# Idle products in TensorE's pauses at the end of a decode step, and the last K transposes and score maximum in halves

## The chip, the cores and the metric

The kernel runs on one core of a Trainium2 chip. Times are microseconds of device time for one execution of the whole program; lower is better.

## The reference

A decode step of one token for a batch of 4, as a sum of the input, an attention block and a gated MLP, both on the layer-normed input:

```python
def _A_ref(x, k_cache, v_cache, wq, wo):          # x (4,1,640)
    q = (x @ wq).reshape(B, Sq, 32, 128).transpose(0, 2, 1, 3)
    scores = einsum('bhqd,bhkd->bhqk', q, k_cache) * 128 ** -0.5   # caches (4,32,4096,128) bf16
    o = einsum('bhqk,bhkd->bhqd', softmax(scores), v_cache)
    return o.transpose(0, 2, 1, 3).reshape(B, Sq, 32 * 128) @ wo   # wo (4096,640)

def _B_ref(x, w_in, w_sp, b_sp, w_out):           # hidden 864 of 1728
    z = gelu(einsum('bsd,df->bsf', x, w_in))
    g = einsum('ts,bsf->btf', w_sp, layernorm(z[..., 864:])) + b_sp
    return einsum('bsf,fd->bsd', z[..., :864] * g, w_out)

return x + _A_ref(layernorm(x), ...) + _B_ref(layernorm(x), ...)
```

Nearly all data is the K and V caches, each 134 MB, read once.

## The kernel before

The 32 heads are cut into four groups of eight. A unit is one group of one batch element: 8.4 MB of K or of V, held in SBUF as 128 rows of 256 positions. There are 16 K units and 16 V units. All loads of units go through SyncE's queue, one instruction a unit (two for the last K unit of the first group and for the last V unit), in a written order: K of the first four, then V and K in turn, and three V units at the end. SBUF has five half-unit places in the tile `kv`; a table says which two each unit gets, and a load waits until what was there has been read.

A K unit is worked off in eight steps (`emit_K`). Each step transposes 32 by 32 blocks with VectorE (`kT`, line 420), and then TensorE multiplies them with the queries (line 431) into the scores `S`, a PSUM tile of two banks (index `i`), with `w` for the two bf16 halves of a word and `e` for two column groups. After the fourth batch element of a group comes `softmax`: `softmax_max` takes the largest score over both banks (line 438), spreads it over the partitions with a product at line 442 and makes its negative; ScalarE takes the exponential (line 476), VectorE transposes the result (line 482), and `z_fill` lays it out on VectorE, ScalarE and GpSimd as stationary operands. `emit_V` then runs 64 products of 512 columns into a PSUM tile `O` (line 503), four of them side by side on the array, and VectorE reduces them to `R`.

At the end, after the last V unit, `emit_sel` gathers `R` by head with eight products (line 527) into a tile of the pool `misc`, which has two buffers; `emit_oT` scales it and writes `oT` with VectorE (line 536). Then come the products with wo (`o_mul`, line 544): 32 chunks, loaded into the place of the next to last V unit in five pieces that end at chunks 12, 20, 28, 31 and 32. The first 20 chunks go into `proj`, the accumulator that already holds the other summands, 320 columns a product, two column groups side by side. VectorE copies and adds `proj`'s parts (lines 582 and 586) while the last twelve chunks go into a second accumulator, `last`, 160 columns a product, 48 products. One addition (line 596) and two stores end the kernel.

Of the kernel before, what the change touches and what calls it, by code (L numbers as in the profile page):

```python
# [9 lines left out]
ALU = mybir.AluOpType  # L10
AX = mybir.AxisListType
F32 = mybir.dt.float32
# [4 lines left out]
def kernel(  # L17
# [19 lines left out]
    nc = tc.nc  # L37
    P = 128
    B, Sq, D = A_x.shape
    _, H, Sk, Dh = A_k_cache.shape  # L40
# [6 lines left out]
    T = Sk // M  # L47
    C2 = 2
    TC = 32
    KW = Dh // 2  # L50
    assert T == C2 * 4 * TC and M == 16 and KW == 64 and H % HG == 0
    NG = H // HG
    NU = NG * B
# [16 lines left out]
    NH = 2  # L70
    NO2 = NOUT // NH
# [4 lines left out]
    small = ctx.enter_context(tc.tile_pool(name="small", bufs=2))  # L76
# [11 lines left out]
    def misc_ps(shape, dtype):  # L88
        misc_ctr[0] += 1
        return ps_m.tile(shape, dtype, tag="misc", name=f"misc{misc_ctr[0]}")  # L90
# [13 lines left out]
    Zb = [w.bitcast(BF16).rearrange("p (a h c) -> p a h c", h=HG, c=4) for w in w_part[2:4]]  # L104
# [66 lines left out]
    def unit(item, t0, t1):  # L171

        s0, s1 = place[item]
        assert s1 == s0 + 1 or t1 <= T // 2 or t0 >= T // 2
        if t0 >= T // 2:
            return at_slot(s1, (t1 - t0) * Dh, t0 * Dh - SL)
        return at_slot(s0, (t1 - t0) * Dh, t0 * Dh)
# [11 lines left out]
    CW = H * Dh // P  # L189
    RQ = Dh // CW  # L190
    wo_t = at_slot(0, CW * NOUT).rearrange("p (c n) -> p c n", c=CW)
# [8 lines left out]
    ident_bf = const.tile([P, P], BF16)  # L200
# [47 lines left out]
    for q in range(4):  # L248
# [10 lines left out]
    SelX = const.tile([P, RQ, HG * RQ], F32)  # L259
# [3 lines left out]
                          in_=SelH[:, None, :].to_broadcast((P, RQ, HG)))  # L263
# [8 lines left out]
    for q in range(4):  # L272
        nc.gpsimd.tensor_copy(out=SelE[32 * q:32 * q + 32, :, q % 2, :],
                              in_=b8[32 * q:32 * q + 32, 8:8 + HP, None].to_broadcast((32, HP, RQ)))
# [10 lines left out]
                          in_=ident_f[:].rearrange("p (q x c) -> p q x c", q=2, c=C2))  # L285


    proj = ps_j.tile([64, 512], F32)
    RW = NH * B
    for hf in range(NH):  # L290
        nc.tensor.matmul(proj[0:32, 0:NO2], lhsT=ident_bf[:XR, 1 - hf:33 - hf],  # L291
                         rhs=x_bf[:, hf * NO2:(hf + 1) * NO2], start=(hf == 0), stop=False)
# [4 lines left out]
    for hf in range(2):  # L297
        for c in range(DC):
            for j in range(NG):
                n0 = j * HG * Dh + hf * 512  # L300
                nc.tensor.matmul(q4_ps[32 * j:32 * j + 32, hf * 512:hf * 512 + 512], lhsT=xnT[:, c, :],  # L301
                                 rhs=wq[:, c, n0:n0 + 512], start=(c == 0), stop=(c == DC - 1))
# [4 lines left out]
    for a in range(2):  # L307
        op = nc.vector.tensor_copy if a == 0 else nc.scalar.copy
# [14 lines left out]
    for (bk, q), names in z_in.items():  # L323
        col, parts = 0, []
        for t in names:
            p0, p1, st, _, n, k, run = PC[t]
            x0, x1 = max(p0, 32 * q), min(p1, 32 * q + 32)
            m = len(range(x0, x1, st)) * n
            assert col + m <= 256
            src = w_z[:, :, :, f_of[t][0]:f_of[t][1]].rearrange("p d a (r i c) -> p d a r i c", i=k, c=run)  # L330
            dst = zr_ps[bk][32 * q:32 * q + 32, :, col:col + m]
# [11 lines left out]
    for c in range(DC):  # L343
        for parts in z_parts:
            for j, (dst, src) in enumerate(parts):
                nc.tensor.matmul(dst, lhsT=xnT[:, c, :], rhs=src[:, c], start=(c == 0 and j == 0),  # L346
                                 stop=(c == DC - 1 and j == len(parts) - 1))
# [4 lines left out]
    for (bk, q, t), (col, m, n, c0, x0, x1, st) in z_at_col.items():  # L352
        rows = slice(32 * q, 32 * q + 32)
        nc.scalar.activation(out=zT[rows, :, c0:c0 + n, x0:x1:st],  # L354
                             in_=zr_ps[bk][rows, :, col:col + m].rearrange("p a (x c) -> p a c x", c=n),
# [37 lines left out]
    for f0 in range(0, FC, 4):  # L393
        for hf in range(NH):
            for fc in range(f0, min(f0 + 4, FC)):
                nb = 32 if fc == 1 and hf == 0 else RW
                u0, r0 = 32 * fc + 1 - hf, 32 * (fc % 2)
                nc.tensor.matmul(proj[r0:r0 + nb, 0:NO2], lhsT=uT[:, u0:u0 + nb],  # L398
                                 rhs=w_out[:, fc, hf * NO2:(hf + 1) * NO2],
                                 start=(fc == 1 and hf == 0), stop=False)  # L400
# [9 lines left out]
    state = {}  # L410

    def emit_K(u, k):

        g, b = divmod(u, B)
        hh = first.get(u, 0) ^ (k // 4)
        qp, kh = k // 2 % 2, k % 2
        t0 = 2 * TC * (2 * hh + qp)
        kw = unit(("k", u), t0, t0 + 2 * TC).bitcast(F32).rearrange("p (t w) -> p t w", w=KW)[:, :, 32 * kh:32 * kh + 32]
        kT = kT_t[:, k % 2]
        nc.vector.transpose(kT.rearrange("p (t r) -> p t r", r=32), kw)  # L420
        if ("S", g) not in state:
            S_new = ps_s.tile([P, 2, TC, M], F32, tag="S", name="S")
            state[("S", g)] = S_new
        S_ps = state[("S", g)]
        kb = kT.bitcast(BF16).rearrange("p (i t e m w) -> p i t e m w", i=2, e=NE, m=M, w=2)
        w0 = 8 - (b * C2 + hh)
        for w in range(2):
            for i in range(2):
                for e in range(NE):
                    q = 2 * qp + e  # L430
                    nc.tensor.matmul(S_ps[32 * q:32 * q + 32, i], lhsT=QZ[:, b, 2 * kh + w, e, w0:w0 + 32],  # L431
                                     rhs=kb[:, i, :, e, :, w], start=(b == 0 and k < 4 and kh == 0 and w == 0),
                                     stop=(b == B - 1 and k >= 4 and kh == 1 and w == 1))

    def softmax_max(g):
        S_ps = state[("S", g)]
        m1 = small.tile([P, 1], F32, tag="m1")
        nc.vector.tensor_reduce(out=m1[:], in_=S_ps[:].rearrange("p i t m -> p (i t m)"), axis=AX.X, op=ALU.max)  # L438
        dg = ppool.tile([P, P], F32, tag="p", name="dg")
        nc.vector.tensor_scalar(out=dg[:], in0=IdF[:], scalar1=m1[:, 0:1], scalar2=None, op0=ALU.mult)  # L440
        mm = misc_ps([P, P], F32)
        nc.tensor.matmul(mm[:], lhsT=ones_f[:], rhs=dg[:], start=True, stop=True)
        mp = small.tile([P, NE * HP * B], F32, tag="mp")
        nc.vector.tensor_reduce(out=mp[:], in_=mm[:].rearrange("p (x c) -> p x c", c=4), axis=AX.X, op=ALU.max)
        mo = small.tile([P, NE * HP * B], F32, tag="mo")
        nc.vector.tensor_tensor(out=mo[:], in0=mp[:], in1=SelN[:].rearrange("p e x -> p (e x)"), op=ALU.mult)
        negmax = small.tile([P, 1], F32, tag="negmax")
        nc.vector.tensor_reduce(out=negmax[:], in_=mo[:], axis=AX.X, op=ALU.add)  # L448
        return negmax
# [45 lines left out]
    def emit_V(v):  # L495
        g, b = divmod(v, B)
        O_ps = ps_o.tile([P, 4, Dh], F32, tag="O", name="O")
        vv = unit(("v", v), 0, T)

        parts = [(qp, x) for x in range(C2) for qp in range(2)] if v == 0 else [(qp, x) for qp in range(2) for x in range(C2)]  # L500
        for w in [w for qp, x in parts for w in range(32 * x + 16 * qp, 32 * x + 16 * qp + 16)]:
            q = w % 4
            nc.tensor.matmul(O_ps[32 * q:32 * q + 32, :, :], lhsT=Zb[b % 2][:, w].rearrange("p h c -> p (h c)"),  # L503
                             rhs=vv[:, w * 4 * Dh:(w + 1) * 4 * Dh], start=(w < 4), stop=(w >= NW - 4))

        if b == 0:
            R_new = small.tile([P, B, Dh], F32, tag="R", name="R", bufs=1)
            state["R"] = R_new
        R = state["R"][:, b, :]
        if v < NU - 1:  # L510
            om4 = ppool.tile([P, 4, Dh], F32, tag="p", name="om4")
            nc.vector.tensor_tensor(out=om4[:], in0=O_ps[:], in1=Mk4[:, :, None].to_broadcast((P, 4, Dh)), op=ALU.mult)  # L512
            nc.vector.tensor_reduce(out=R, in_=om4[:].rearrange("p c d -> p d c"), axis=AX.X, op=ALU.add)  # L513
        else:
            nc.vector.tensor_scalar(out=R, in0=O_ps[:, 0, :], scalar1=Mk4[:, 0:1], scalar2=None, op0=ALU.mult)  # L515
            for c in range(1, 4):
                nc.vector.scalar_tensor_tensor(out=R, in0=O_ps[:, c, :], scalar=Mk4[:, c:c + 1], in1=R,
                                               op0=ALU.mult, op1=ALU.add)
        if b + 2 < B:
            z_fill(g, b + 2)  # L520

    def emit_sel(g):

        ox = misc_ps([P, B, CW], F32)
        r0 = 32 * g
        for d in range(RQ):
            nc.tensor.matmul(ox[r0:r0 + 32], lhsT=SelX[:, d], rhs=state["R"][:, :, d * CW:(d + 1) * CW],  # L527
                             start=(d == 0), stop=(d == RQ - 1))
        state[("ox", g)] = ox

    oT = const.tile([P, CW * RW + 32], BF16)
# [8 lines left out]
    def o_mul(dst, c, hf, n0, n1, start, stop):  # L540

        nb = 32 if start else RW
        c0 = RW * c + 1 - hf
        nc.tensor.matmul(dst[0:nb, 0:n1 - n0], lhsT=oT[:, c0:c0 + nb], rhs=wo_t[:, c, n0:n1], start=start, stop=stop)  # L544

    fill_qz(0)
    for w in w_part[2:4]:
# [3 lines left out]
    for i, item in enumerate(seq):  # L551
# [6 lines left out]
        g, b = divmod(u, B)  # L558
# [11 lines left out]
                softmax(g)  # L570
        else:
            emit_V(u)
    emit_sel(NG - 1)
    emit_oT(NG - 1)

    CL = 20
    for c in range(0, CL, 2):
        for hf in range(NH):
            for p in range(2):
                o_mul(proj[32 * p:32 * p + 32], c + p, hf, hf * NO2, (hf + 1) * NO2, False, c == CL - 2 and hf == NH - 1)  # L580
    o_1 = ppool.tile([32, NO2], F32, tag="p", name="o_1")
    nc.vector.tensor_copy(out=o_1[:], in_=proj[0:32, 0:NO2])
    NQ = NO2 // 2
# [5 lines left out]
    for c in range(CL, CW):  # L589
        for hf in range(NH):  # L590
            for k in range(2):
                n0 = hf * NO2 + k * NQ
                o_mul(last[32 * k:32 * k + 32], c, hf, n0, n0 + NQ, c == CL and hf == 0, c == CW - 1 and hf == NH - 1)

    o_bf = ppool.tile([64, NQ], BF16, tag="p", name="o_bf")
    nc.vector.tensor_tensor(out=o_bf[:], in0=last[:], in1=o_q[:], op=ALU.add)
# [31 lines left out]
```

## Time and profile before

| | |
|---|---|
| median of 3 runs | 663.94 us (663.32 to 664.98) |
| the profiled execution: own time, span | 664.68 us, 662.8 us |
| busy: PE, DVE, ACT, POOL | 291.6, 371.6, 74.8, 76.4 us |
| data moved, mean rate | 282.60 MB, 426 GB/s |
| mean granted TensorE clock | 0.722 |
| K transposes (L420), 128 of them | 282.6 us, 2274 ns each |
| score products (L431), 1024 | 187.9 us |
| V products (L503), 1024 | 76.3 us |
| largest score (L438), 4 | 4.9 us, 1225 ns each |

The span runs from the first to the last instruction of the program that the profiler recorded; the own time is that of the same execution as the device reports it, and is 1.88 us longer. Busy times say how long an engine worked, not whether anything waited for it. The granted clock is the share of TensorE's clock pulses that were let through.

### The profile page before, as it was taken

How to read it: one execution, taken by the hardware profiler on the slowest of the kernel's cores; microseconds unless marked ns; L12 is line 12 of the kernel's file. 1: busy time of each engine (PE TensorE's matmuls, PEld its weight loads, DVE VectorE, ACT ScalarE, POOL GpSimd, SP SyncE). 2: the span in 40 equal slices, each digit the busy share in tenths (PEclk: the TensorE clock that was granted, in tenths of full speed). 3: DMA queues.
4: the chain of work that ended last, by engine and by line, in shares of the span. 5: the costliest groups of instructions: out<-in, count | busy, mean ns of one | idle time of the engine just before them, and what ended most of it. 6: DMA issues, size and time to landing. Idle time of an engine off the chain costs nothing.

```text
span 662.8 us, 5648 instructions
## 1 busy us (share of the span) xinstructions
PE 291.6 (44%) x2361; PEld 112.0 (17%) x2361; DVE 371.6 (56%) x304; ACT 74.8 (11%) x144; POOL 76.4 (12%) x136
## 2 busy tenths in 40 slices
PE   0436566447063452536344270644426064436254
PEld 0222211112021120112111020211102021112023
DVE  5239999756191744779173461978446191773011
ACT  0310000431000000060200000052200000026100
POOL 7440000031100000030300000022300000004100
PEclk9857879768587685877768586767859577686567
DMA  9999999999999999999999999999999999999996
GB/s 370 443 442 440 410 448 421 435 440 443 424 439 420 435 440 427 432 425 435 436 435 432 435 431 436 427 432 424 436 443 431 432 423 428 443 440 435 410 420 256
DMA packets 6370, 282.60 MB, mean 426 GB/s; under 512 B 1036, under 2 KB 1172, under 8 KB 1304
## 3 DMA queue, kind: packets, MB, share of 16 engines
q1 hardware_dynamic: 5950, 281.60, 98.5%
q0 software_dynamic: 368, 0.65, 0.3%
q8 instruction: 18, 0.29, 0.2%
q14 instruction: 6, 0.05, 0.0%
q10 hardware_dynamic: 28, 0.01, 0.0%
HBM read 282.25 MB, written 0.01 MB: 426 GB/s over the span
## 4 chain that ended last, share of the span: by engine, by line
DMA 69%; DVE 12%; issue 12%; PE 4%; POOL 1%; ACT 1%; SPq 0%; DVEq 0%; POOLq 0%; ACTq 0%
DMA kv<-in_A_k_cache_dram 58%; DVE w_words L420 11%; DMA kv<-in_A_wo_dram 4%; DMA kv<-in_A_v_cache_dram 4%; DMA kv<-in_B_w_in_dram 4%; PE O L503 2%; PE proj L398 1%; PE last L544 1%; POOL kv L382 0%; PE misc L346 0%; ACT kv L354 0%; DVE w_words L482 0%; PE S L431 0%; POOL z_b L384 0%; DVE w_words L464 0%
## 5 line engine op out<-in xcount | busy, mean ns | idle before, releaser
L420 DVE STREAM_TRANSPOSE w_words<-kv 128x2048 f32<-128x2048 f32 x128 | 282.6, 2274 | 132.5 <-DMA kv<-in_A_k_cache_dram 130.3
L431 PE MATMUL S<-w_words,QZ 128*32 128x512 bf16 x1024 | 187.9, 500 | 259.6 <-DVE w_words L420 259.6
L431 PEld LDWEIGHTS <-QZ 128*32 128x32 bf16 x1024 | 59.8, 110 | 384.4 <-issue 338.1
L503 PE MATMUL O<-kv,w_words 128*32 128x512 bf16 x1024 | 76.3, 463 | 44.3 <-DMA kv<-in_A_v_cache_dram 29.1
L468 ACT ACTIVATE w_words<-w_words,MkE 32x128 bf16<-32x128 bf16 x120 | 61.0, 508 | 87.5 <-PE O L503 74.2
L512 DVE TENSOR_TENSOR om<-O,Mk 128x512 f32<-128x512 f32 x15 | 10.4, 692 | 82.7 <-PE O L503 82.6
L466 POOL TENSOR_SCALAR w_words<-w_words,MkE 32x128 bf16<-32x128 bf16 x60 | 42.9, 715 | 109.2 <-PE O L503 104.5
L476 ACT ACTIVATE w_words<-S,negmax 128x1024 bf16<-128x1024 f32 x4 | 4.5, 1113 | 423.8 <-DVE negmax L448 423.8
L503 PEld LDWEIGHTS <-w_words 128*32 128x32 bf16 x1024 | 33.9, 113 | 86.7 <-issue 56.4
L406 POOL COPY QZ<-qT 32x32 bf16<-32x32 bf16 x16 | 5.0, 316 | 286.1 <-PE S L431 285.5
L464 DVE TENSOR_SCALAR w_words<-w_words,MkE 32x128 bf16<-32x128 bf16 x76 | 25.4, 334 | 2.4
L513 DVE TENSOR_REDUCE R<-om 128x128 f32<-128x512 f32 x15 | 15.3, 1020 | 0.5
L487 POOL TENSOR_SCALAR rs<-MkB,rowsum 128x4 f32<-128x4 f32 x4 | 1.2, 297 | 122.2 <-ACT w_words L476 122.2
L482 DVE STREAM_TRANSPOSE w_words<-w_words 128x1024 bf16<-128x1024 bf16 (+1 forms) x8 | 9.6, 1241 | 5.9 <-ACT w_words L476 5.9
L398 PE MATMUL proj<-w_words,z_b 128*8 128x320 bf16 (+1 forms) x52 | 5.7, 398 | 8.8 <-DVE z_b L385 8.8
L438 DVE TENSOR_REDUCE m<-S 128x1 f32<-128x1024 f32 x4 | 4.9, 1225 | 6.2 <-PE S L431 6.2
L527 PE MATMUL misc<-R,SelX 128*32 128x128 f32 x32 | 4.2, 276 | 7.2 <-DVE R L513 5.5
L515 DVE TENSOR_SCALAR R<-O,Mk 128x128 f32<-128x128 f32 x1 | 0.3, 350 | 12.4 <-PE O L503 12.4
L301 PE MATMUL q<-kv,xnT 128*32 128x512 bf16 x40 | 3.9, 567 | 6.3 <-DVE xnT L228 6.3
L544 PEld LDWEIGHTS <-oT 128*8 128x8 bf16 (+1 forms) x88 | 5.0, 109 | 5.5 <-issue 4.2
L490 PE MATMUL misc<-rs,SelE 128*32 128x4 f32 x8 | 1.1, 206 | 10.7 <-POOL rs L487 10.7
L291 PE MATMUL proj<-kv,ident_bf 8*32 8x320 bf16 x2 | 0.7, 442 | 10.6 <-DMA kv<-in_A_x_dram 10.6
(100 smaller groups left out, 87.7 us busy)
## 6 DMA issues: line engine op xcount, KB each, us to landing
kv<-in_A_k_cache_dram SPq DMA_DIRECT2D x2, 4096.0 KB
kv<-in_A_v_cache_dram SPq DMA_DIRECT2D x1, 6144.0 KB
kv<-in_A_wq_dram SPq DMA_DIRECT2D x1, 5120.0 KB, 16.2
kv<-in_A_wo_dram SPq DMA_DIRECT2D x2, 1280.0 KB
kv<-in_B_w_in_dram SPq DMA_DIRECT2D x1, 2160.0 KB, 23.8
kv<-in_A_v_cache_dram SPq DMA_DIRECT2D x1, 2048.0 KB
kv<-in_A_wo_dram SPq DMA_DIRECT2D x1, 1920.0 KB, 22.2
kv<-in_A_wo_dram SPq DMA_DIRECT2D x1, 480.0 KB, 25.5
```

The lines of the kernel that those rows point to most:

```text
L398: nc.tensor.matmul(proj[r0:r0 + nb, 0:NO2], lhsT=uT[:, u0:u0 + nb], rhs=w_out[:, fc, hf * NO2:(hf + 1) * NO2], start=(fc == 1 and hf == 0) ...
L406: nc.gpsimd.tensor_copy(out=QZ[r0:r0 + 32, :, :, :, 8 + 8 * hp], in_=qT[32 * g:32 * g + 32, NE * hp:NE * hp + NE].rearrange("p e a b -> p ...
L420: nc.vector.transpose(kT.rearrange("p (t r) -> p t r", r=32), kw)
L431: nc.tensor.matmul(S_ps[32 * q:32 * q + 32, i], lhsT=QZ[:, b, 2 * kh + w, e, w0:w0 + 32], rhs=kb[:, i, :, e, :, w], start=(b == 0 and k < ...
L464: nc.vector.tensor_scalar(out=dst, in0=src, scalar1=mk, scalar2=None, op0=ALU.mult)
L466: nc.gpsimd.tensor_scalar(out=dst, in0=src, scalar1=mk, scalar2=None, op0=ALU.mult)
L468: nc.scalar.activation(out=dst, in_=src, func=ACT.Copy, scale=mk)
L482: nc.vector.transpose(pT_t[:, j0:j1, :], blocks)
L503: nc.tensor.matmul(O_ps[32 * q:32 * q + 32, :, :], lhsT=Zb[b % 2][:, w].rearrange("p h c -> p (h c)"), rhs=vv[:, w * 4 * Dh:(w + 1) * 4 * ...
L512: nc.vector.tensor_tensor(out=om4[:], in0=O_ps[:], in1=Mk4[:, :, None].to_broadcast((P, 4, Dh)), op=ALU.mult)
L513: nc.vector.tensor_reduce(out=R, in_=om4[:].rearrange("p c d -> p d c"), axis=AX.X, op=ALU.add)
L544: nc.tensor.matmul(dst[0:nb, 0:n1 - n0], lhsT=oT[:, c0:c0 + nb], rhs=wo_t[:, c, n0:n1], start=start, stop=stop)
```

## The change

- `keep_busy` issues products of 512 columns from the identity and the last V unit into a PSUM tile `idle` that nothing reads: four behind the last V product, two behind the selecting products, four behind the chunk before 12 and five behind the chunk before 20. `tc.issue_after` fixes the order on TensorE: each is queued behind the product named, and the following real products behind the last of them.
- For the last step of the last batch element of each group, `emit_K` transposes in two halves, and the products of the first bank are issued between the two.
- `softmax_max` takes the maximum of each bank by itself into `m2` and then the larger of the two.

```diff
@@ emit_K
         kT = kT_t[:, k % 2]
-        nc.vector.transpose(kT.rearrange("p (t r) -> p t r", r=32), kw)
+        kT_v = kT.rearrange("p (i t r) -> p i t r", i=2, r=32)
+        halves = b == B - 1 and k == 7
+        if not halves:
+            nc.vector.transpose(kT.rearrange("p (t r) -> p t r", r=32), kw)
...
-        for w in range(2):
-            for i in range(2):
+        for x in range(2):
+            if halves:
+                nc.vector.transpose(kT_v[:, x], kw[:, TC * x:TC * x + TC])
+            for y in range(2):
+                w, i = (y, x) if halves else (x, y)
                 for e in range(NE):
@@ softmax_max
-        nc.vector.tensor_reduce(out=m1[:], in_=S_ps[:].rearrange("p i t m -> p (i t m)"), axis=AX.X, op=ALU.max)
+        m2 = small.tile([P, 2], F32, tag="m2")
+        for i in range(2):
+            nc.vector.tensor_reduce(out=m2[:, i:i + 1], in_=S_ps[:, i].rearrange("p t m -> p (t m)"), axis=AX.X, op=ALU.max)
+        nc.vector.tensor_tensor(out=m1[:], in0=m2[:, 0:1], in1=m2[:, 1:2], op=ALU.max)
@@ the end (emit_V and emit_sel keep their last product in state["mm"], o_mul returns its product)
-    emit_sel(NG - 1)
+    idle = misc_ps([P, 4 * Dh], F32)
+
+    def keep_busy(n, behind):
+
+        for _ in range(n):
+            with tc.issue_after(behind.ins):
+                behind = nc.tensor.matmul(idle[:], lhsT=ident_bf[:], rhs=unit(("v", NU - 1), 0, T)[:, 0:4 * Dh],
+                                          start=True, stop=True)
+        return behind
+
+    behind = keep_busy(4, state["mm"])
+    with tc.issue_after(behind.ins):
+        emit_sel(NG - 1)
+    behind = keep_busy(2, state["mm"])
     emit_oT(NG - 1)
...
-                o_mul(proj[32 * p:32 * p + 32], c + p, hf, hf * NO2, (hf + 1) * NO2, False, c == CL - 2 and hf == NH - 1)
+                with tc.issue_after(behind.ins):
+                    behind = o_mul(proj[32 * p:32 * p + 32], c + p, hf, hf * NO2, (hf + 1) * NO2, False,
+                                   c == CL - 2 and hf == NH - 1)
+        if c + 2 in (12, CL):
+            behind = keep_busy(4 if c + 2 < CL else 5, behind)
...
-                o_mul(last[32 * k:32 * k + 32], c, hf, n0, n0 + NQ, c == CL and hf == 0, c == CW - 1 and hf == NH - 1)
+                with tc.issue_after(behind.ins):
+                    behind = o_mul(last[32 * k:32 * k + 32], c, hf, n0, n0 + NQ, c == CL and hf == 0,
+                                   c == CW - 1 and hf == NH - 1)
```

More of the change, by code (lines that the diff above doesn't have):

```diff
@@ L502, in emit_V @@
             q = w % 4
-            nc.tensor.matmul(O_ps[32 * q:32 * q + 32, :, :], lhsT=Zb[b % 2][:, w].rearrange("p h c -> p (h c)"),
+            state["mm"] = nc.tensor.matmul(O_ps[32 * q:32 * q + 32, :, :], lhsT=Zb[b % 2][:, w].rearrange("p h c -> p (h c)"),
                              rhs=vv[:, w * 4 * Dh:(w + 1) * 4 * Dh], start=(w < 4), stop=(w >= NW - 4))
@@ L526, in emit_sel @@
         for d in range(RQ):
-            nc.tensor.matmul(ox[r0:r0 + 32], lhsT=SelX[:, d], rhs=state["R"][:, :, d * CW:(d + 1) * CW],
+            state["mm"] = nc.tensor.matmul(ox[r0:r0 + 32], lhsT=SelX[:, d], rhs=state["R"][:, :, d * CW:(d + 1) * CW],
                              start=(d == 0), stop=(d == RQ - 1))
@@ L543, in o_mul @@
         c0 = RW * c + 1 - hf
-        nc.tensor.matmul(dst[0:nb, 0:n1 - n0], lhsT=oT[:, c0:c0 + nb], rhs=wo_t[:, c, n0:n1], start=start, stop=stop)
+        return nc.tensor.matmul(dst[0:nb, 0:n1 - n0], lhsT=oT[:, c0:c0 + nb], rhs=wo_t[:, c, n0:n1], start=start, stop=stop)
     fill_qz(0)
```

## The prediction

> **What bounds the kernel now.** I read the page's slices first, then the chain of waits for the end, then the timeline of TensorE there, and last the windows view cut along the steps of the granted clock. The row of DMA digits:
>
> ```profile
> DMA  9999999999999999999999999999999999999996
> ```
>
> All slices but the last are full: the kernel streams 282.6 MB at 426 GB/s, and what is not behind the last landing is hidden. The chain of waits from 630 us on:
>
> ```profile
> 631.44 0.43 issue
> 631.87 24.71 DMA kv<-in_A_wo_dram
> 656.58 0.04 issue
> 656.62 3.40 PE last L544 x48
> 660.02 0.02 issue
> 660.05 0.32 DVE o_bf L596
> ```
>
> The third piece of wo lands at 656.58; then 48 products (3.40 us), one addition, the store. The fourth and fifth pieces land at 657.77 and 658.16 (the trace's landing events). So after the last byte has landed there are 1.9 us of products still to run. The timeline of TensorE, with the idle time in brackets:
>
> ```profile
> 650.43 1.80 PE L544 MATMUL proj<-kv,oT 128*8 128x320 bf16 x24 [1.07 <-DMA kv<-in_A_wo_dram]
> 653.53 1.26 PE L544 MATMUL proj<-kv,oT 128*8 128x320 bf16 x16 [1.29 <-DMA kv<-in_A_wo_dram]
> 656.62 3.39 PE L544 MATMUL last<-kv,oT 128*32 128x160 bf16 x48 [1.84 <-DMA kv<-in_A_wo_dram]
> ```
>
> The proj products take 320 columns in 75 ns each (1.80/24), the last ones 160 columns in 71 ns each (3.39/48): half the width, the same time. The windows view says why (columns: us, busy time and count of PE, PEld, DVE, ACT, POOL, then granted clock, DMA share, GB/s):
>
> ```profile
> 645.43:648.84 3.41, 1.79 (x29) 1.06 (x22) 1.40 (x4) 0.00 (x0) 0.00 (x0) 1.00 1.02 427
> 648.84:652.25 3.41, 2.32 (x29) 1.48 (x28) 0.31 (x1) 0.00 (x0) 0.00 (x0) 1.00 1.00 419
> 652.25:655.67 3.42, 1.26 (x16) 0.77 (x16) 0.80 (x3) 0.00 (x0) 0.00 (x0) 1.00 0.99 411
> 655.67:659.08 3.41, 2.46 (x38) 2.46 (x39) 0.31 (x1) 0.00 (x0) 0.00 (x0) 0.50 0.27 105
> 659.08:662.49 3.41, 0.93 (x14) 0.59 (x10) 0.32 (x1) 0.00 (x0) 0.00 (x0) 0.50 0.01 2
> ```
>
> The clock steps only on a grid of 3.41 us. It was 1.00 for the proj products and 0.50 for the last 48, and the window before the step had TensorE busy for 1.26 us, 37%. Windows earlier in the trace give the limits:
>
> ```profile
> 502.07:505.48 3.41, 1.60 (x13) 0.43 (x9) 3.41 (x2) 0.00 (x0) 0.00 (x0) 1.00 0.84 365
> 505.48:508.90 3.42, 2.00 (x16) 0.76 (x15) 2.48 (x2) 0.00 (x0) 0.00 (x0) 1.00 1.24 537
> ...
> 543.03:546.44 3.41, 1.54 (x12) 0.43 (x8) 3.41 (x2) 0.00 (x0) 0.00 (x0) 1.00 0.84 365
> 546.44:549.85 3.41, 3.13 (x24) 1.16 (x27) 0.23 (x1) 0.00 (x0) 0.00 (x0) 0.50 1.16 500
> ...
> 594.23:597.64 3.41, 2.04 (x20) 0.89 (x24) 3.09 (x11) 3.26 (x7) 0.00 (x0) 0.50 0.84 365
> 597.64:601.05 3.41, 3.41 (x36) 1.44 (x32) 2.49 (x7) 3.23 (x8) 1.50 (x3) 0.50 1.20 519
> 601.05:604.46 3.41, 0.86 (x16) 0.23 (x8) 1.71 (x2) 3.26 (x7) 3.05 (x5) 1.00 0.80 346
> ```
>
> At full clock a window with 1.60 us busy (47%) keeps it, one with 1.54 (45%) loses it; at half clock 2.04 (60%) does not bring it back, 3.41 does. All windows of the trace fit: full clock is held from about 45% on, and regained from about 82%.
>
> **Part 1, the fifteen idle products.** Each is 512 columns over the whole array. The nearest row is the attention-times-V products (L503), four of which share the array: a group of four starts every 0.216 us at full clock and every 0.427 at half. So a filler costs 0.216 or 0.427. At full clock, in the order of the queue:
> - Four behind the last V product: its issue ends at 646.52, the four run to 647.39. The selecting products wait for VectorE's R until 648.30: hidden, 0.9 us to spare.
> - Two behind the selecting products: 649.17 to 649.6, and the next product waits for wo's first piece, landed at 650.39: hidden.
> - Four behind chunk 11: 652.06 to 652.93, and the second piece lands at 653.49: hidden, 0.5 us to spare.
> - Five behind chunk 19: 654.62 to 655.70, and the third piece lands at 656.58: hidden, 0.9 us to spare. VectorE's copy of proj waits for the real product ahead of them.
>
> With a drain of 0.17 us each, the window 652.25 to 655.67 gets 1.26 + 0.85 + 0.89 = 3.0 us busy, 88% instead of 37%, and the two before it 78% and 81%. So the clock stays at 1.00 at 655.67.
>
> The last 48 then go at full clock. The proj pairs start every 0.135 us for 320 columns, so 160 columns give 0.069 us a pair, 34.6 ns each. Bounds: at best this, at worst the 66.7 ns they take now, should something other than columns pace them; I take 34.6 since the products into misc at L346 were issued at 36 ns each (80 in 2.9 us) even at half clock, each with its own weights. Then 32 products: 656.62 + 1.11 = 657.73; wait for the fourth piece, 657.81; 12 products to 658.22; the fifth piece has landed; 4 products, the last starting at 658.33 and taking 0.23 (0.299 of a proj product less 0.067 for 160 columns): 658.56. Now the last one ends at 660.01. Gain 1.45 us, and it can't pass 1.6, as four products, 0.1 of starts and 0.23 of drain stand behind the landing at 658.16.
>
> A rule of the Trainium skill speaks against this price: "TensorE: Matmul & The Clock Gate", Back-to-back issue gap, gives some 81 ns a product for a stream of weight load and matmul at 128 columns. By it the 48 would take 3.9 us and nothing would be gained; the trace disagrees, with 71 ns now at half clock and 36 ns at L346.
>
> **Part 2, the last K transposes in halves.** One of 2.17 us becomes two of about 1.1, four times in the kernel. Four products for the first half run under the second transpose, and four instead of eight stand behind it: 1.13 us becomes about 0.6. **Part 3, the largest score in halves.** From the rows of 128 elements (0.29) and 1024 (1.23) a reduce of 512 is 0.69; the first runs beside the second four products, then 0.69 and a small op of 0.19 (as L446). Transposes' end to maximum: now 585.62 to 588.05, 2.43 us; then some 0.1 for the second start, 0.04 + 0.69 + 0.03 + 0.69 + 0.03 + 0.19, 1.8 us. Bounds 1 us saved to 0.5 lost, should the halves still wait for each other. On the path: nothing. All it can bring forward is the first V product of the group, which ends at 601.95 and frees the place for a V load; that load is queued behind one that lands at 606.7, a cover of 4.7 us. If that cover were gone, each such us would cost one us, four times. ScalarE, GpSimd and VectorE's later work only start sooner, with no transfer to collide with.
>
> **Sum.** Profiled execution: span 662.8, own time 664.68, so 1.88 lies around it. 664.68 - 1.45 = **663.2**. This execution is 0.74 above the median of 663.94. The grid does not start with the kernel. If I shift it through one period and apply the two limits to the same intervals, the before kernel keeps the full clock at the end in about half of the positions, as an estimate; the runs from 663.32 to 664.98, 1.66 apart, look like both kinds. The change should bring all runs to the kind of the fastest: 0.7 below the median, or 0.1%.
>
> **Rivals.**
> 1. *Something other than columns paces the last 48.* A weight load shows 87 ns at full clock in the proj stage; if two loads in one column group could not overlap, a pair takes 0.087 and the 48 end at 658.9 (gain 1.1); if issue binds at today's 67 ns, the gain is 0. Time 663.6 to 664.7. Against it: L346. 10%.
> 2. *There is no clock to be won*, because only gaps of a whole window cost it, and the step at 655.67 had another cause, or the timed runs mostly hold the clock already. Time 663.9, the median. Against: gaps of 1.07, 1.29 and 1.84 us were followed by 0.50. The same page's section on HAM oscillation asks only for no gap over some 3.4 us; by that rule these gaps cost nothing, which this trace contradicts with its 37% window. 14%.
> 3. *Slower: the fillers run at half clock ahead of the real products.* If the clock falls before chunk 19 ends, five take 2.13 us, from 654.62 to 656.75, and hold back products that were free at 656.62; the four after chunk 11 end 0.24 late too. All 48 are slow as now: 664.68 + 0.15 = 664.8, 0.9 above the median. It decides if the granted clock is 0.50 between 652 and 655.7. To pass 0.3% it would need 2 us, ten times that. 5%.
> 4. *More than 0.3% faster*: under 661.95, which the landing at 658.16 forbids unless the stream itself ends over a us sooner. 6%.
>
> The forecast has the remaining 65%. A measurement of this kernel tells some 0.3%, 2.0 us, from no change; the forecast and the first three rivals all lie inside. So: within 0.3% 0.87, faster 0.09 (rival 4 and the lucky end of the forecast), slower 0.04 (rival 3 with a disturbed stream). The range runs from 0.5 below the forecast, for the spread of the landings, to 664.3, which takes in rival 2 and most of rival 1.
>
> **What would show it.** Right: granted clock 1.00 up to the store; the group of 48 from 3.39 to about 1.9 us, its last products waiting for the landing of wo and not for TensorE; the fillers inside the old idle gaps; span near 661.3; V loads landing as before although the scores' maximum is ready about 0.6 us sooner. Wrong: clock 1.00 with a pair still at 0.13 us (rival 1); clock 0.50 at the last 48 (rivals 2, 3); a start of those 48 after 656.62 by the landing's clock (rival 3); a slice of DMA under 9 in mid-kernel.

## The result, and the profile after

The changed kernel takes 663.33 us (median of 13 runs, 662.26 to 663.66); the kernel before, run beside it, 664.88 (13 runs, 663.32 to 665.95). The ratio is 0.9977, with a 95% interval of 0.9969 to 0.9986: 1.5 us, 0.2%, within the 0.3% of the forecast and on the side it named. The profiled execution has a span of 660.6 and its own time is 662.51.

The chain of waits at the end, as shown for before:

```profile
631.12 24.74 DMA kv<-in_A_wo_dram
655.86 0.04 issue
655.90 1.93 PE last L553 x48
657.83 0.02 issue
657.86 0.32 DVE o_bf L624
```

Two numbers moved: the 48 products take 1.93 us instead of 3.40, and the third piece of wo lands at 655.86 instead of 656.58. The first is the clock. The timeline of TensorE (line 588 is the idle products; one record of the five is missing):

```profile
647.80 1.06 PE L536 MATMUL misc<-R,SelX 128*32 128x128 f32 x8 [0.64 <-DVE R L526]
...
649.73 1.80 PE L553 MATMUL proj<-kv,oT 128*8 128x320 bf16 x24 [0.33 <-DMA kv<-in_A_wo_dram]
651.46 1.04 PE L588 MATMUL misc<-kv,ident_bf 128*128 128x512 bf16 x4
652.82 1.25 PE L553 MATMUL proj<-kv,oT 128*8 128x320 bf16 x16 [0.33 <-DMA kv<-in_A_wo_dram]
654.24 1.03 PE L588 MATMUL misc<-kv,ident_bf 128*128 128x512 bf16 x4 [0.16 <-issue]
655.90 1.92 PE L553 MATMUL last<-kv,oT 128*32 128x160 bf16 x48 [0.64 <-DMA kv<-in_A_wo_dram]
```

Each group of fillers ends before the landing that the next real products wait for: the gaps in brackets before real products still end with DMA or VectorE, never with an idle product. The windows on this execution's grid:

```profile
650.33:653.74 3.41, 3.08 (x36) 1.67 (x34) 0.00 (x0) 0.00 (x0) 0.00 (x0) 1.00 1.01 426
653.74:657.15 3.41, 2.61 (x44) 1.68 (x41) 1.11 (x3) 0.00 (x0) 0.00 (x0) 1.00 0.72 288
657.15:660.56 3.41, 0.67 (x18) 0.46 (x15) 0.32 (x1) 0.00 (x0) 0.00 (x0) 1.00 0.01 2
```

90% and 77% busy, and a granted clock of 1.00 to the end. The last piece lands at 657.44 and the last product ends at 657.82, 0.38 behind it; before, 658.16 and 660.01, 1.85 behind. That is 1.47 us. The other 0.7 of the span's 2.2 is the stream, which the prediction had not touched.

This one profile does not show that the idle products held the clock. Counting the real products alone, the first two of these windows are 62% and 47% busy, and by the prediction's limit of about 45% that would have held it too: the grid happened to lie well. What the idle products do has to be read from the times of many runs and from the runs below.

### The profile page after: what moved, and what is told of

Its sections match the earlier page's. It is cut to its first block, busy times and chain, and to the rows that moved or that the text cites. A ratio compares the mean times of both kernels' runs of the same rounds, so it can differ in the third digit from the quotient of the medians.

```text
span 660.6 us, 5688 instructions
## 1 busy us (share of the span) xinstructions
PE 277.7 (42%) x2374; PEld 108.0 (16%) x2376; DVE 372.2 (56%) x316; ACT 74.8 (11%) x144; POOL 76.7 (12%) x136
## 4 chain that ended last, share of the span: by engine, by line
DMA 70%; DVE 12%; issue 12%; PE 4%; POOL 1%; ACT 1%; SPq 0%; DVEq 0%; POOLq 0%; ACTq 0%
DMA kv<-in_A_k_cache_dram 58%; DVE w_words L423 11%; DMA kv<-in_A_v_cache_dram 4%; DMA kv<-in_A_wo_dram 4%; DMA kv<-in_B_w_in_dram 4%; PE O L512 2%; PE proj L398 1%; POOL kv L382 0%; ACT kv L354 0%; PE misc L346 0%; DVE w_words L491 0%; DVE w_words L432 0%; POOL z_b L384 0%; PE last L553 0%; PE S L437 0%
## 5 line engine op out<-in xcount | busy, mean ns | idle before, releaser
L423 DVE STREAM_TRANSPOSE w_words<-kv 128x2048 f32<-128x2048 f32 x124 | 273.7, 2275 | 136.7 <-DMA kv<-in_A_k_cache_dram 133.7
L437 PE MATMUL S<-w_words,QZ 128*32 128x512 bf16 x1024 | 175.8, 471 | 269.5 <-DVE w_words L423 267.5
L437 PEld LDWEIGHTS <-QZ 128*32 128x32 bf16 x1024 | 57.4, 107 | 386.2 <-issue 334.0
L512 PE MATMUL O<-kv,w_words 128*32 128x512 bf16 x1024 | 71.1, 438 | 49.3 <-DMA kv<-in_A_v_cache_dram 34.3
L432 DVE STREAM_TRANSPOSE w_words<-kv 128x1024 f32<-128x1024 f32 x8 | 9.3, 1204 | 0.0
L446 DVE TENSOR_REDUCE m<-S 128x1 f32<-128x512 f32 x8 | 5.2, 686 | 3.0 <-PE S L437 3.0
L451 PE MATMUL misc<-dg,ones_f 128*128 128x128 f32 x8 | 2.3, 376 | 7.7 <-DVE dg L449 7.7
```

The source lines that it names most:

```text
L432: nc.vector.transpose(kT_v[:, x], kw[:, TC * x:TC * x + TC])
L446: nc.vector.tensor_reduce(out=m2[:, i:i + 1], in_=S_ps[:, i].rearrange("p t m -> p (t m)"), axis=AX.X, op=ALU.max)
L512: state["mm"] = nc.tensor.matmul(O_ps[32 * q:32 * q + 32, :, :], lhsT=Zb[b % 2][:, w].rearrange("p h c -> p (h c)"), rhs=vv[:, w * 4 * Dh: ...
```

## The experiments

The theory: (a) the fillers gain by holding the clock over the last 48 products, and (b) the halves, off the path, gain nothing. The rivals: products paced otherwise, an effect of gaps or counts instead of busy share, or a stream that the halves do shorten.

**The fillers alone.** `emit_K` and `softmax_max` as before, the rest as changed.

```diff
-            if halves:
-                nc.vector.transpose(kT_v[:, x], kw[:, TC * x:TC * x + TC])
+        nc.vector.transpose(kT.rearrange("p (t r) -> p t r", r=32), kw)
...
-            nc.vector.tensor_reduce(out=m2[:, i:i + 1], in_=S_ps[:, i].rearrange("p t m -> p (t m)"), axis=AX.X, op=ALU.max)
+        nc.vector.tensor_reduce(out=m1[:], in_=S_ps[:].rearrange("p i t m -> p (i t m)"), axis=AX.X, op=ALU.max)
```

> The fifteen idle products stay; the last transposes and the score maximum are whole again. If the gain is the clock at the end: time as the changed kernel (ratio to before 0.9977, some 1.5 us below before), granted clock 1.00 under the last 48 products, group of 48 about 1.9 us, last product some 0.4 us behind wo's last landing. If the halves brought part of it: ratio between 0.998 and 1.000, and the last landing some 0.2 to 0.7 us later after the start than in the changed kernel.

Measured: 663.91 us (12 runs), ratio 0.9993 (0.9983 to 1.0004), the second of the two cases. The end is as expected: clock 1.00, the 48 in 1.87 us, the last product 0.4 us behind the last landing. But wo's third piece lands at 657.25, not 655.86, 1.4 us later where 0.2 to 0.7 was expected. So the clock at the end may not be the whole gain.

**The halves alone.**

```diff
-    behind = keep_busy(4, state["mm"])
...
-    behind = keep_busy(2, state["mm"])
...
-            behind = keep_busy(4 if c + 2 < CL else 5, behind)
```

> No idle products; the halves of the transposes and of the maximum stay. If the halves are hidden behind the stream: ratio to before 1.000 within 0.0007, last 48 products 3.2 to 3.4 us in an execution whose clock steps to 0.50 there, and 1.9 in one where it doesn't. If they shorten the stream: ratio 0.999 or less and the last landing sooner than 658.2.

Measured: 664.24 us, ratio 0.9994 (0.9982 to 1.0005): not told from no change by itself, and the last landing, 658.49, is not sooner than 658.2. By its own expectation this run spoke for hidden halves. The end is that of before:

```profile
652.53:655.95 3.42, 1.34 (x18) 0.77 (x16) 0.71 (x2) 0.00 (x0) 0.00 (x0) 1.00 0.99 411
655.95:659.36 3.41, 2.34 (x36) 2.33 (x37) 0.40 (x2) 0.00 (x0) 0.00 (x0) 0.50 0.24 92
```

39% busy in the window, then 0.50 and 3.40 us for the 48.

The twelve times fall into two groups: six from 663.25 to 663.87 and six from 664.61 to 665.50.

**Only the five behind chunk 19.**

```diff
-    behind = keep_busy(4, state["mm"])
+    behind = keep_busy(0, state["mm"])
...
-    behind = keep_busy(2, state["mm"])
+    behind = keep_busy(0, state["mm"])
...
-        if c + 2 in (12, CL):
-            behind = keep_busy(4 if c + 2 < CL else 5, behind)
+        if c + 2 == CL:
+            behind = keep_busy(5, behind)
```

> Of the fifteen only the five behind chunk 19 stay. If the clock goes by the busy share of a 3.41 us window (45% keeps it): the window before the last products has 1.26 + 0.9 = 2.1 us busy, 63%, so the clock holds and the time is that of the changed kernel, 0.9977 of before. If what counts is that no gap is left open (gaps of 1.07 and 1.29 us are back): half clock returns in part of the runs, ratio 0.999.

Measured: 663.45 us, ratio 0.9979 (0.9968 to 0.999), 12 runs from 662.41 to 663.80. The windows:

```profile
650.51:653.93 3.42, 2.13 (x31) 1.19 (x28) 0.00 (x0) 0.00 (x0) 0.00 (x0) 1.00 1.01 426
653.93:657.34 3.41, 2.76 (x49) 1.91 (x49) 1.11 (x3) 0.00 (x0) 0.00 (x0) 1.00 0.67 266
```

The gaps of 1.61, 0.88 and 1.28 us are open again and the clock holds. In this profile the grid lies well again: without the five, the second window would be 46% busy. The times decide. Apart from the fixed order of issue, this kernel differs from the halves alone by the five only, and all twelve runs are in the range of its lower group or under it. Ten of the fifteen idle products are not needed.

The profiles agree. All three without idle products at the end (before, the halves alone, and before once more, further below) lost the clock there; all ten with some kept it. In one of the ten, the last run of this section, the real products alone fill 39% of the window before the step at 657.75; with the five it is 74%, and the clock stays at 1.00 under the 48 products, which run from 656.91 to 658.82:

```profile
654.33:657.75 3.42, 2.52 (x38) 1.45 (x36) 1.11 (x3) 0.00 (x0) 0.00 (x0) 1.00 0.59 230
657.75:661.16 3.41, 1.06 (x30) 0.79 (x24) 0.32 (x1) 0.00 (x0) 0.00 (x0) 1.00 0.01 3
```

**Fifteen narrow ones**, 32 columns instead of 512.

```diff
-  nc.tensor.matmul(idle[:], ..., rhs=unit(("v", NU - 1), 0, T)[:, 0:4 * Dh],
+  nc.tensor.matmul(idle[:, 0:32], ..., rhs=unit(("v", NU - 1), 0, T)[:, 0:32],
```

> The fifteen idle products stay in their places but have 32 columns instead of 512, about 0.03 us each. If the busy share counts: they add 0.3 us at most to a window, which stays near 37 to 45%, and the time goes back to that of before, ratio 0.999 to 1.000. If the number of products or the length of gaps counts: gain as with the full ones, 0.9977.

Measured: 663.71 us, ratio 0.9984 (0.9973 to 0.9995), runs from 662.37 to 665.25. The expectation missed: the gain is between the two. A group of them shows 0.22 to 0.29 us with its drain, so a window of 37% comes to 44% and more, right at the limit, and the wide spread fits a clock held in some runs only. Its profile can't decide: there the grid falls so that the two windows before the last products have 2.27 and 2.33 us busy. So this run does not tell share from count or gaps. Windows of the profiles do. In the prediction's lines, 13 products at 47% kept the clock and 16 at 37% lost it, so the count is not what decides. For gaps, a window of the kernel before and one of the changed kernel, each with the one behind it:

```profile
78.81:82.22 3.41, 1.29 (x10) 0.55 (x12) 3.19 (x2) 0.00 (x0) 0.00 (x0) 1.00 0.86 368
82.22:85.64 3.42, 1.61 (x8) 0.34 (x4) 1.96 (x1) 0.00 (x0) 0.00 (x0) 0.50 1.02 441
```
```profile
599.13:602.54 3.41, 1.45 (x28) 0.54 (x20) 2.14 (x4) 3.23 (x8) 3.05 (x5) 1.00 0.98 423
602.54:605.96 3.42, 0.00 (x0) 0.00 (x0) 0.00 (x0) 1.93 (x4) 2.15 (x4) 1.00 1.15 498
```

The first has no gap over 1.07 us, is 38% busy and loses the clock; the second stands idle for its last 2.0 us, is 43% busy and keeps it.

**Sixteen instead of five behind chunk 19.**

```diff
-            behind = keep_busy(4 if c + 2 < CL else 5, behind)
+            behind = keep_busy(4 if c + 2 < CL else 16, behind)
```

> Sixteen instead of five idle products behind chunk 19, all else as in the changed kernel. Eleven more at 0.216 us are 2.4 us; 1.0 us of the idle time before the third piece is left to hide them, so the last 48 products start 1.2 to 1.4 us late (some 0.2 us a product beyond the fifth and a half), at full clock: ratio to the changed kernel 1.002, to before about 0.9995 to 1.0005. If the fillers gave way to real products: no loss, 0.9977.

Measured: 665.08 us, ratio 1.0007 (0.9996 to 1.0018). The timeline:

```profile
653.65 1.25 PE L553 MATMUL proj<-kv,oT 128*8 128x320 bf16 x16 [0.33 <-DMA kv<-in_A_wo_dram]
654.84 3.63 PE L588 MATMUL misc<-kv,ident_bf 128*128 128x512 bf16 x16
658.40 1.84 PE L553 MATMUL last<-kv,oT 128*32 128x160 bf16 x48
```

The third piece landed at 656.70; the products start 1.7 us later (1.2 to 1.4 was expected), at once behind the fillers, with no idle time before them. The 16 take 3.5 us at 0.216 each. This is the delay that rival 3 feared, here at full clock: a filler costs nothing up to the landing and its full length after it, and sixteen give back all of the gain.

**The kernel before once more**, unchanged, for a second profile.

> The kernel before under another name, for a second profile of it. If the grid of 3.41 us does not start with the kernel: its steps lie elsewhere in the span than in the first profile, and the last 48 products take 3.4 us (clock 0.50 when they start) or 1.9 us (1.00), with the clock following the 45% share of the window before. If the grid starts with the kernel: steps at 645.4, 648.8, 652.3 and 655.7 again and 3.4 us. Ratio 1.000.

Measured: 664.74 us, ratio 0.9999 (0.9986 to 1.0012). The grid lies elsewhere and the rule holds in both directions:

```profile
654.34:657.76 3.42, 1.25 (x16) 0.76 (x16) 1.11 (x3) 0.00 (x0) 0.00 (x0) 1.00 0.88 361
657.76:661.17 3.41, 2.80 (x44) 2.80 (x45) 0.00 (x0) 0.00 (x0) 0.00 (x0) 0.50 0.09 35
```

37% busy loses the clock; the next window, 82% busy at half clock, regains it at 661.17, so the 48 take 3.18. But this execution's third piece landed at 658.32, 1.7 us after the first profile's. The stream itself differs.

**The changed kernel and the fillers alone again**, both unchanged, on one chip.

> The changed kernel again, beside the fillers alone on one chip. If the halves bring nothing: ratio to before equal to that of the fillers alone within their intervals, both 0.997 to 0.999, and in both profiles the last product ends 0.4 us behind the last landing of wo; what differs between runs is when wo lands. If the halves shorten the stream: this one stays at 0.9977 and the fillers alone at 0.9993.

> The fillers alone a second time, to tell a matter of the program from one of the run. If the later landing of the first time (658.8 instead of 657.4) was the run's: landing between 657.4 and 658.3, ratio 0.998. If it belongs to the program: landing at 658.7 again, ratio 0.999 again.

Measured: 663.49 us, ratio 0.9988 (0.9976 to 1.0), and 663.87 us, ratio 0.9981 (0.9969 to 0.9994). The two ratios don't part them, and neither comes out at the 0.9977 and 0.9993 of the first time. The medians of all runs do better: 663.36 for 25 runs of the changed kernel, 663.91 for 24 of the fillers alone, a difference of 0.3 to 0.8 as a 95% interval from resampling the runs. With 664.24 for the halves alone and 664.8 for the kernel before, the fillers are worth some 0.9 us with or without the halves, and the halves some 0.5 with or without the fillers, though without the fillers the runs spread too widely to tell. The landings differ as well: third piece at 656.08 with the halves, at 657.41 without, as it was the first time.

So the halves seem to shorten the stream, by about half a us in time. The profiles alone can't show it, for the halves and the place of the grid come mixed in them. The grids of the kernel before, of the halves alone and of both profiles of the fillers alone lie within 0.3 us of one another. Among these four the halves bring nothing at the second group: its first V products start at 286.33 with them and at 286.31 to 286.34 without, for the last step's score products ran at half clock in all four. In the five profiles that have both halves and fillers and nothing else that bears on the groups, the grid lies elsewhere, the clock was at 1.00 there, and these products start at 285.57 to 285.90.

Where: at the group boundaries the next V load waits until the first V unit's 64 products have been done. From the timeline of the kernel before, of its second profile, and of the changed kernel: TensorE's line of the 64 products, and on SyncE's queue the load that they release.

```profile
286.31 5.65 PE L503 MATMUL O<-kv,w_words 128*32 128x512 bf16 x64 [3.83 <-DVE w_words L464]
292.00 0.33 SPq L186 DMA_DIRECT2D kv<-in_A_v_cache_dram  x1
```
```profile
286.70 6.49 PE L503 MATMUL O<-kv,w_words 128*32 128x512 bf16 x64 [3.82 <-DVE w_words L464]
293.24 0.33 SPq L186 DMA_DIRECT2D kv<-in_A_v_cache_dram  x1
```
```profile
285.57 5.07 PE L512 MATMUL O<-kv,w_words 128*32 128x512 bf16 x64 [3.82 <-DVE w_words L473]
290.69 0.33 SPq L186 DMA_DIRECT2D kv<-in_A_v_cache_dram  x1
```

Worked out from the trace's DMA packets, the stream's lowest rate in a us there (434 GB/s otherwise) is 398 with the load out at 292.00, 314 at 293.24, 418 at 290.69; the fillers alone have 392 at 292.09 and 392 at 292.07, the halves alone 367 at 292.15. The load that the stream still has ahead is waited for until 296.4 to 296.7 in all of these. With 3.3 to 4.5 us of cover, then, the packets under way at once fell from 16.0 to between 13.0 and 15.2 in the worst us: some of the 16 DMA engines ran dry all the same. With the changed kernel's 5.8 us they stayed at 16.0.

Summed over the three boundaries at 292, 446 and 602, what falls short of 434 GB/s is worth 0.2 to 0.3 us in the five profiles with halves and fillers, 0.5 to 0.7 in the first profile of before, the halves alone and the fillers alone, and 1.8 in the second profile of before. The mean landing of wo's fourth piece over the 16 engines goes along with it: 656.39 to 656.44, 656.72 to 656.94, and 657.80. Three runs test this.

**A later maximum**, one more reduction over the whole score tile a group.

```diff
+        m0 = small.tile([P, 1], F32, tag="m0")
+        nc.vector.tensor_reduce(out=m0[:], in_=S_ps[:].rearrange("p i t m -> p (i t m)"), axis=AX.X, op=ALU.max)
         m2 = small.tile([P, 2], F32, tag="m2")
```

> The changed kernel with one more maximum over the whole score tile per group, result unused: 1.23 us later to the exponential. Theory of the dry engines: the V loads at 291, 446 and 601 go out 1.2 us later, dips as deep as in the second profile of before, wo lands 0.4 to 1.2 us later, ratio to before 0.9985 to 1.000. Rival, a cover of 4.7 us as in the prediction: no change, 0.998, landing at 657.1 to 657.7.

Measured: 664.74 us, ratio 1.0 (0.9985 to 1.0015): the whole gain is gone, though the end holds its clock (the 48 in 1.92 us). Loads go out at 292.67, 448.67 and 603.74 (changed: 290.69, 446.41, 600.63); the rate falls to 358, 321 and 395; the third piece lands at 659.18. The loads are 2.0 to 3.1 us later where 1.2 was expected, and the landing 3.1 to 3.3 where 0.4 to 1.2 was. That profile is of one of its slowest executions, 666.46, and at the boundary shown below half clock under the last score products adds to the extra reduction. The mean rate over 20 us, changed kernel and this one (last column, GB/s):

```profile
284.00:304.00 20.00, 9.39 (x88) 3.66 (x89) 14.89 (x24) 10.70 (x22) 5.79 (x8) 0.72 1.01 437
```
```profile
284.00:304.00 20.00, 9.83 (x84) 3.63 (x86) 16.50 (x26) 11.18 (x22) 5.70 (x8) 0.67 0.97 411
```

**Idle products between scores and V**, twenty a group, on the changed kernel and on the fillers alone. `fill_gap` is `keep_busy` with 512 columns of `kT` as its moving operand; five stand behind the last score product, six behind the product of the maximum, nine behind that of the row sums.

```diff
+        behind = fill_gap(warm, 5, state["s_mm"])
...
+            behind = nc.tensor.matmul(mm[:], lhsT=ones_f[:], rhs=dg[:], start=True, stop=True)
+        state["s_mm"] = fill_gap(warm, 6, behind)
...
+            behind = nc.tensor.matmul(cs[r0:r0 + 32, :], lhsT=SelE[:].rearrange("p h e q -> p (h e q)"), rhs=rs4[:],
+                                      start=True, stop=True)
+        state["s_mm"] = fill_gap(warm, 9, behind)
```

> The changed kernel plus twenty idle products a group between the last score products and the first V products. Theory: the first V load of a group boundary is issued only when 64 V products are done, and where that comes late some DMA engines run dry (418 instead of 434 GB/s at 293 us in the changed kernel, 314 in the second profile of before). With the clock held, the 64 take 3.5 to 4.5 us instead of 5.0 to 6.3, the loads go out 1 to 2 us sooner, the dips at 293 and 449 vanish, wo lands by 657.2, and the time is 0 to 0.4 us below the changed kernel. Rival: the queue covers it, no dip matters, time and landing as the changed kernel. If the fillers run at half clock they hold back the first V products: later by up to 1 us a group.

> The fillers alone (transposes and maximum whole) plus the twenty idle products a group. If what the halves bring is only that V products end sooner: this gives it back, wo lands near 657.4 instead of 658.8 and 658.9, ratio 0.997 to 0.998. If the halves act in another way: landing stays near 658.8, ratio 0.9985 to 0.999.

Measured: 663.36 us, ratio 0.9979 (0.9967 to 0.9991), and 663.62 us, ratio 0.9987 (0.9976 to 0.9998).

```profile
285.51 3.73 PE L529 MATMUL O<-kv,w_words 128*32 128x512 bf16 x64 [1.82 <-DVE w_words L485]
289.29 0.33 SPq L186 DMA_DIRECT2D kv<-in_A_v_cache_dram  x1
```

With the clock held, the 64 products take 3.7 us, the loads go out at 289.29 and 290.18, and from 289 to 298 and from 446 to 454 no us is under 430 GB/s. So the dips go as the theory says. The landing and the time do not follow as expected. On the changed kernel nothing more is won, and wo's last piece lands at 658.27, not by 657.2: the mean landing of the fourth piece was 656.39 already and is 656.46 here, and the latest of the 16 engines sets the time, 657.06 there and 657.88 here. Without halves the last piece lands at 658.44, nearer to the 658.8 and 658.9 of the fillers alone than to 657.4, and the ratio is in the range of the second case. The mean landing of the fourth piece, 656.62 against 656.78 and 656.94, and the median, 663.62 against 663.91 on another chip, are only somewhat better. So taking the dips away gave back only a part of what the halves bring; the rest is open. No version beats the changed kernel clearly.

## Why the prediction was right, and where it was not

- **The last 48 products** were put at 656.62 to 658.56, 1.94 us; measured 1.93. A pair starts every 0.069 us. Rival 1 is out. The row that the price leaned on, L346, was weaker support than it looked, as its products have 16 to 184 columns, 98 on average. The Trainium skill's 81 ns a product at 128 columns ("TensorE: Matmul & The Clock Gate", Back-to-back issue gap) does not hold here: with 160 columns and a weight load each it is 34.5 ns a product, 69 in each of the two column groups.
- **The share rule** held at the end of every profile: 37% and 39% lost the clock, 62% kept it, 82% regained it. Its limits are less sharp than "all windows of the trace fit" says. In that trace itself the clock was regained at 77% and 80% (windows from 24.20 and 440.63) and not regained at 83% (from 416.73); over all thirteen profiles it was lost at up to 46% and held from 41%, kept at half up to 83% and regained from 76%. Rival 2 is out: the share told what came next and the gaps did not. The Trainium skill's rule of no idle gaps over some 3.4 us ("TensorE: Matmul & The Clock Gate", HAM oscillation) is not enough here, as the clock was also lost in a window without a gap over 1.07 us.
- **The fillers' cover** was right in all four places; its edge is where sixteen showed it.
- **The sum** of 663.2 met a median of 663.33, but by luck in part: two errors cancel. It took the full 1.45 us off the profiled execution, while the fillers alone gained 0.9 in the medians (664.8 to 663.9), as the kernel before holds its clock in some executions; the halves, put at nothing, made up the rest. And the forecast of 0.7 below the median of three runs, 663.94, became 1.5 below that of thirteen, 664.88.
- **The step that failed** is "On the path: nothing" for the halves. By the times they bring about 0.5 us. The prediction took the next landing at 606.7 as a cover of 4.7 us, as if the queue were one pipe; it is 16 engines, and loads issued 3.3 to 4.5 us ahead of the landing at 296.5 already cost rate. That this is all of the 0.5 us is not shown.
- **The halves' size** was wrong too. The first reduction was to run beside the second products. VectorE's timeline after shows that it doesn't:

```profile
582.75 2.33 DVE L432 STREAM_TRANSPOSE w_words<-kv 128x1024 f32<-128x1024 f32 x2
585.82 1.29 DVE L446 TENSOR_REDUCE m<-S 128x1 f32<-128x512 f32 x2 [0.74 <-PE S L437]
```

The reductions start 0.74 behind the transposes, when all products are done. The negative maximum comes 3.86 us behind the transposes against 4.07 in the last group, 0.2 sooner instead of 0.6. In the earlier groups it is 3.9 to 4.2 against 4.2 to 5.1, but there the clock differs too: it was 1.00 behind the transposes in all four groups of the changed kernel's profile, and half for part of that time in two groups of the profile of before. Over all profiles that tell, the maximum takes 3.9 to 4.2 us with the halves and 4.1 to 4.3 without where the clock was full, and 4.4 to 4.6 against 4.6 to 5.2 where half clock fell in. The prediction had priced full clock alone.

The lag of single engines is left open. With no dip at all, the sixteen landings of the last piece spread over 2.3 to 2.7 us (1.5 in the changed kernel's profile), and that spread moves the end by several tenths of a us from run to run. Instruction fetches of 16 KB take some 1.05 us of one engine each (a data packet of 64 KB takes 2.4), 18 in the kernel; whether they set the lag was not tested.

## What to carry to other kernels

When a stretch of products ends the kernel, cut the windows view along the steps of the granted clock and read the busy share of the window before: a few idle products in the last gap may hold the clock, and one group at the right place does what four do. Count each filler from its issue to the landing that the real work waits for: up to there it is free, beyond it is paid in full. And before calling a step hidden behind a full stream, look for rates a few per cent lower after the loads that the step releases: cover on the mean landing is not cover on every engine.

## What the runs showed of the hardware

- The clock's grid of 3.41 us lay at different places in the profiles, so runs of one kernel can differ by the 1.5 us that half clock costs here; the stream's landings add to that. The 25 runs of the changed kernel lie within 2.4 us, 35 of before on one chip within 3.4.
- The clock followed the busy share of TensorE in one window of the grid. It was lost at 38% without a gap over 1.07 us and kept at 43% with 2.0 us of idle time at one stretch; it was kept with 13 products at 47% and lost with 16 at 37%.
- A load queued 4.5 us before the one ahead of it is in (292.09 against 296.57) still let the stream fall from 434 to 392 GB/s.
